# Counting the filler products of TensorE's first gap from the moment when the rows they read exist: 30 matrices in place of 54

## The chip, the core and the metric

The kernel runs on one core of a Trainium2 chip. The metric is device time in microseconds (us) of one execution of the whole program. Before the change three executions took 694.41, 691.67 and 690.75 us, so the median is 691.67 us. Beside them stands one profiled execution, whose trace is what the rest of this document reads.

The core's engines run their own instruction streams in order and wait for each other on semaphores: TensorE (PE in the profile, with its weight loads shown as PEld), VectorE (DVE), ScalarE (ACT), GpSimd (POOL), and SyncE (SP), which here only issues DMAs. DMAs are also issued by POOL and ACT.

## The reference

Two blocks follow each other. The first is a gated recurrence over 768 time steps with a complex decay per channel; batch is 4, there are 8 heads, and the head dimension is 48:

```
scale = min(|a|, 0.999) / (|a| + 1e-6);  a_n = a * scale
S_t = a_n[t] * S_{t-1} + k[t] v[t]^T        (complex state, 48 x 48 per head)
y[t] = q[t] . Re(S_t)
```

The second is a SwiGLU feed-forward on the 3072 rows of the result, each with 384 features (8 heads x 48): an RMS norm with a gain, two matrices 384 x 1536 (`w_gate`, `w_val`), `silu(g) * val`, and one matrix 1536 x 384 (`w_out`). All of it is fp32.

## The kernel before, in words

**Tiling.** The sequence is cut into chunks of 128 steps: 4 x 6 = 24 chunks, numbered n = 0 to 23. Gates are worked out in units: chunks 0 and 1 alone, then pairs of chunks. The feed-forward takes groups of two chunks (256 rows).

**Stages of a chunk.** `load_gates` and `load_kq` (lines 1091 and 1117) fetch the gates `in` and the queries and keys `kin`. `gates` (line 1138) turns the gates into cumulated magnitudes and phases on DVE and ACT and multiplies queries and keys by them: the results are the rows `rot` (one DVE product each for cosine and sine). SP then moves each chunk's `rot` by six DMAs into `kq`, in the layout that the attention needs. `attend` (line 1247) does one chunk's attention on PE: scores (`bank<-kq`, 64 products for a chunk), whose causal part DVE copies into `am`; transposes of the keys (`ident,kq`), copied by ACT into `kt`; the chunk's output (`am,ve` and `kq,state`); the new state (`vn,kt`, 48 products), finished by DVE; and the norm (`ones,sq`, then a power on POOL written to `rs`, spread again by PE as `ident,rs`), after which DVE writes `xT`. `feed` (line 1381) multiplies a group's `xT` by `wg` and `wv`. The values of a chunk are loaded twice, as `ve` and as `vn`; there is one buffer of `vn`, so that the next chunk's load of it waits for the state products of the chunk before.

**The weights** arrive in the inputs' 64-bit form, in pieces of 1536 KB that POOL's DMA queue fetches into the buffers `wo` and `hT` (`fetch`, line 1012). A piece is turned into fp32 by one ACT pass and three DVE passes (`narrow`, line 1035). At most two pieces are under way. Piece 4 (`wo<-in_w_gate_dram` for the second time) also waits until the second chunk's `kq` has landed: POOL reads one element of it (`seen<-kq`), and this read stands on POOL behind the first chunk's power `rs`.

**The order.** Nothing is issued as it is written. Every operation is put down with an engine, an estimated duration, its dependencies and a due time (class `Flow`). `schedule` (line 617) plays the program through with these estimates, engine by engine, and so finds the order in which each engine issues its instructions; `issue` (line 741) emits them in that order. On the chip an engine follows its own order and waits for the semaphores of what it depends on. The planned times themselves are not enforced.

**Fillers.** Where PE would idle in the plan's first 62 us (`WARM`), `schedule` puts products whose result nobody reads (lines 706 to 713): 128x128 by 128x128 in fp32, of the rows `rot` of chunk 0, into a bank of PSUM that is not in use. How many there are comes from the planned gap: its length, less a margin of 0.25 us, by 0.26 us for each. In the trace each of these matrices shows as two MATMUL records. They can't begin before the rows `rot` are written, as they read them. `started` (line 1222) holds one operation, the DVE product that writes those rows; `since` (line 708) is the planned time from which the gap is counted. `recent` is a list of what PE did lately; in the plan, two small groups of products for the decays of chunks 0 and 1 (`bank<-ot,ot`) stand before the first gap, so the list isn't empty there. The fillers stand in PE's stream just ahead of the operation that the plan puts after the gap: here the scores of chunk 0.

Of the kernel before, what the change touches and what calls it, by code (L numbers as in the profile page):

```python
# [500 lines left out]
class Flow:  # L501
# [115 lines left out]
    def schedule(self):  # L617
# [3 lines left out]
        free = {}  # L621
# [10 lines left out]
        recent = []  # L632
# [13 lines left out]
        while True:  # L646
# [58 lines left out]
                dur += self.between(o, last)  # L705
                mode, last = o["mode"], o
            if eng == "PE" and self.warm and not claimed and t < self.warm["until"] and all("end" in x for x in self.warm["after"]):
                since = max([free["PE"]] + [x["end"] + 0.06 for x in self.warm["after"] if not recent])
                step = 0.26 if recent else 0.43
                n = int((t - since - 0.25) / step)  # L710
                if n > 0:
                    self.fillers.append((order - 0.5, n))
                    recent.append((since, since + step * n))
# [1039 lines left out]
```

## Time and profile before

| | before |
|---|---|
| median of three executions | 691.67 us |
| profiled execution | 691.83 us |
| its span | 690.1 us |
| granted TensorE clock, mean | 0.996 |
| busy: PE, DVE, ACT, POOL | 652.9, 556.2, 499.6, 63.7 us |
| bytes moved by DMA | 81.98 MB |

The span runs from the first to the last instruction of the profiled execution; 1.73 us of its own time lie around it. Times in the views count from the span's start. A row of the timeline gives start, duration, engine, the line of the program (746, the line of `issue` from which all is emitted), the operation, what it writes and reads, its shapes and how many like it follow each other; in brackets stands how long the engine was idle before it and what ended that. The duration of a merged row reaches from the first start to the last end. `SPq` and `POOLq` rows are DMA issues: their duration is the issue, not the transfer.

### The profile page before, as it was taken

The page shows a single profiled execution, that of the slowest core. Times are in us where ns is not written, and L with a number is a line of the kernel's source. Part 1 is how long each engine was busy: PE and PEld are TensorE (multiplying, and loading weights), DVE is VectorE, ACT ScalarE, POOL GpSimd, SP SyncE. Part 2 cuts the span into 40 slices and gives each one's busy share as a digit, 9 for nine tenths or more (in the row PEclk, how much of TensorE's full clock was granted, in tenths as well). Part 3 has the DMA queues.
Part 4 walks back from the last instruction along what each step waited for, and adds up shares of the span by engine and source line. Part 5 has one row for each costly group of instructions (what it writes and reads, how often), then busy time and mean ns, then how long its engine had stood idle before and what let it go on. Part 6 is the DMA issues. An engine that isn't in the chain of part 4 may idle for free.

```text
span 690.1 us, 19118 instructions
## 1 busy us (share of the span) xinstructions
PE 652.9 (95%) x7965; PEld 609.6 (88%) x7965; DVE 556.2 (81%) x1026; ACT 499.6 (72%) x864; POOL 63.7 (9%) x109
## 2 busy tenths in 40 slices
PE   0699999999999999999999999989999998999997
PEld 0688887786899999999999999989999998999997
DVE  8969999989998969879989869779879777346563
ACT  8629667895685774874788776867679675799872
POOL 3113031011000100011010100101000000000000
PEclk9999999999999999999999999999999999999999
DMA  9786574355325521354552622556151445735510
GB/s 282 257 230 195 146 208 140 98 128 107 102 54 97 140 34 54 92 117 79 141 89 61 146 53 45 115 107 143 39 107 34 95 128 116 258 95 184 161 47 26
DMA packets 104156, 81.98 MB, mean 119 GB/s; under 512 B 41953, under 2 KB 94561, under 8 KB 104065
## 3 DMA queue, kind: packets, MB, share of 16 engines
q1 hardware_dynamic: 98560, 64.68, 35.0%
q0 software_dynamic: 4416, 15.35, 10.5%
q8 instruction: 63, 1.03, 0.6%
q10 hardware_dynamic: 1088, 0.69, 0.3%
q14 instruction: 29, 0.23, 0.1%
HBM read 55.84 MB, written 4.72 MB: 88 GB/s over the span
## 4 chain that ended last, share of the span: by engine, by line
PE 76%; DVE 8%; issue 4%; SPq 4%; DMA 4%; ACT 3%; POOL 0%; DVEq 0%; POOLq 0%; ACTq 0%
PE bank L746 76%; SPq L746 4%; DVE turns L746 1%; DVE hT L746 1%; DVE t L746 1%; DMA decay<-ends 1%; ACT in L746 1%; ACT t L746 1%; DMA in<-in_w_val_dram 1%; DMA ve<-in_v_dram 1%; DVE rot L746 1%; DVE am L746 1%; ACT L746 1%; DMA vn<-in_v_dram 1%; ACT bank L746 1%
## 5 line engine op out<-in xcount | busy, mean ns | idle before, releaser
L746 PE MATMUL bank<-wo,hT 128*128 128x192 f32 (+1 forms) x696 | 140.7, 350 | 0.0
L746 PEld LDWEIGHTS bank<-wo,hT 128*128 128x128 f32 x696 | 115.0, 190 | 11.6 <-DVE hT L746 0.5
L746 PE MATMUL bank<-xT,wg 128*128 128x128 f32 (+1 forms) x488 | 85.3, 308 | 0.0
L746 PE MATMUL bank<-xT,wv 128*128 128x128 f32 (+1 forms) x488 | 83.2, 303 | 0.0
L746 ACT ACT_TABLE_LOAD x57 | 73.1, 1283 | 9.4 <-DVE rot L746 5.1
L746 ACT ACTIVATE hT<-bank 128x512 f32<-128x512 f32 x100 | 58.4, 596 | 25.0 <-PE bank L746 22.5
L746 PEld LDWEIGHTS bank<-xT,wg 128*128 128x128 f32 x488 | 71.4, 193 | 5.3 <-issue 0.6
L746 PEld LDWEIGHTS bank<-xT,wv 128*128 128x128 f32 x488 | 70.6, 193 | 3.2 <-issue 0.2
L746 POOL TENSOR_TENSOR rs<-ssv,mhalf 128x1 f32<-128x1 f32 x24 | 21.4, 890 | 461.5 <-ACT ssv L746 407.9
L746 DVE COPY_PREDICATED am<-causal,bank 128x512 f32<-128x512 int32 x48 | 34.7, 731 | 22.9 <-PE bank L746 22.8
L746 DVE TENSOR_TENSOR hT<-hT 128x768 f32<-128x768 f32 (+1 forms) x60 | 51.5, 860 | 0.4
L746 PE MATMUL bank<-yg,wg 128*128 128x128 f32 x320 | 50.7, 281 | 0.0
L746 PE MATMUL bank<-yg,wv 128*128 128x128 f32 x320 | 48.8, 275 | 0.0
L746 ACT ACTIVATE bank<-bank 128x512 f32<-128x512 f32 x60 | 35.2, 586 | 17.9 <-PE bank L746 11.4
L746 ACT ACTIVATE sg<-bank 128x256 f32<-128x256 f32 (+1 forms) x72 | 38.5, 536 | 9.2 <-DVE bank L746 4.7
L746 DVE TENSOR_TENSOR hT<-bank,hT 128x512 f32<-128x512 f32 x50 | 34.3, 687 | 13.4 <-ACT bank L746 5.3
L746 PE MATMUL bank<-sums,hT 128*128 128x192 f32 x240 | 44.7, 329 | 0.0
L746 PEld LDWEIGHTS bank<-yg,wg 128*128 128x128 f32 x320 | 42.2, 191 | 1.3 <-issue 0.2
L746 PEld LDWEIGHTS bank<-yg,wv 128*128 128x128 f32 x320 | 42.2, 192 | 0.0
L746 PEld LDWEIGHTS bank<-kq 96*32 96x32 f32 x1536 | 30.5, 110 | 11.2 <-issue 5.1
L746 PEld LDWEIGHTS bank<-sums,hT 128*128 128x128 f32 x240 | 39.1, 190 | 0.4 <-DVE mid L746 0.2
L746 PE MATMUL bank<-kq 96*32 96x128 f32 (+3 forms) x1536 | 36.4, 237 | 3.1 <-DMA decay<-ends 1.9
(217 smaller groups left out, 1451.5 us busy)
## 6 DMA issues: line engine op xcount, KB each, us to landing
kq<-rot SPq DMA_DIRECT2D x84, 128.0 KB, 2.5
kq<-kin SPq DMA_DIRECT2D x60, 128.0 KB, 2.6
kin<-in_q_dram SPq DMA_DIRECT2D x24, 192.0 KB, 2.9
kin<-in_k_dram SPq DMA_DIRECT2D x24, 192.0 KB, 3.3
in<-in_a_re_dram SPq DMA_DIRECT2D x11, 384.0 KB, 4.2
in<-in_a_im_dram SPq DMA_DIRECT2D x11, 384.0 KB, 4.2
out_dram<-ot SPq DMA_DIRECT2D x22, 192.0 KB, 3.0
vn<-in_v_dram SPq DMA_DIRECT2D x20, 192.0 KB, 3.2
```

The source lines that it names most:

```text
L746: fn(*args, **kw)
```

## The change

In `schedule` one condition is taken out of the line that finds the start of a gap. Before, the end of the operations in `started`, plus 0.06 us, counted only if the list `recent` was empty. Now it counts always: a gap starts when PE is free and the rows that the fillers read are there, whichever is later.

```diff
@@ -705,7 +705,7 @@
             if eng == "PE" and self.warm and not claimed and t < self.warm["until"] and all("end" in x for x in self.warm["after"]):
-                since = max([free["PE"]] + [x["end"] + 0.06 for x in self.warm["after"] if not recent])
+                since = max([free["PE"]] + [x["end"] + 0.06 for x in self.warm["after"]])
                 step = 0.26 if recent else 0.43
                 n = int((t - since - 0.25) / step)
                 if n > 0:
```

The emitted program has 30 filler matrices in the first gap in place of 54. The fillers of later gaps and the order of everything else are the same.

## The prediction, as it was made before the changed kernel ran

> **What bounds the kernel now.** I read first which engine is busy in which stretch. Columns of the stretches: from and to, then busy time and count of instructions for PE, PEld, DVE, ACT and POOL, granted clock, DMA share, GB/s.
>
> ```profile
> span 690.1 us, 19118 instructions
> 17.00:25.70 8.70, 2.22 (x13) 2.03 (x13) 7.59 (x15) 8.04 (x10) 1.69 (x3) 1.00 1.02 392
> 25.70:40.00 14.30, 14.30 (x112) 14.18 (x116) 8.96 (x9) 3.55 (x5) 1.70 (x2) 1.00 0.55 141
> 40.00:56.00 16.00, 13.57 (x372) 12.21 (x372) 13.97 (x14) 8.30 (x18) 5.17 (x6) 1.00 0.96 252
> 56.00:82.70 26.70, 26.70 (x171) 24.45 (x170) 26.52 (x37) 20.97 (x26) 5.30 (x4) 1.00 0.53 160
> 200.00:690.00 490.00, 480.03 (x5940) 463.10 (x5939) 375.61 (x741) 355.81 (x640) 29.50 (x47) 1.00 0.41 100
> ```
>
> From 56 us on PE sets the pace (26.70 of 26.70 us, then 480.03 of 490), and in the first of these stretches DVE is as full (26.52). PE is full in 25.70 to 40.00 as well, but there it runs fillers, and DVE (8.96 of 14.30) and ACT (3.55) stand idle. So I look at what they wait for. First PE's timeline:
>
> ```profile
> 25.70 14.31 PE L746 MATMUL bank<-rot 128*128 128x128 f32 x108 [6.37 <-DVE rot L746]
> 39.94 1.33 PE L746 MATMUL bank<-kq 96*32 96x128 f32 x64
> ...
> 42.98 0.86 PE L746 MATMUL bank<-vn,kt 128*32 128x48 f32 x48
> ...
> 45.14 1.33 PE L746 MATMUL bank<-kq 96*32 96x128 f32 x64
> 47.30 0.38 PE L746 MATMUL bank<-ident,rs 128*128 128x128 f32 x1 [0.82 <-POOL rs L746]
> ...
> 52.49 0.82 PE L746 MATMUL bank<-vn,kt 128*32 128x48 f32 x43
> 54.51 0.28 PE L746 MATMUL bank<-vn,kt 128*32 128x48 f32 x5 [1.19 <-issue]
> ```
>
> The fillers are 108 records, two for each of 54 matrices. They begin when DVE has written `rot`, 6.37 us after PE became free, and hold PE until 39.94, when chunk 0's scores start. Now the other engines in that time, and last one row of the chain of waits:
>
> ```profile
> 25.67 3.82 SPq L746 DMA_DIRECT2D kq<-rot  x6
> 31.61 0.49 POOL L746 COPY seen<-kq 96x1 f32<-96x1 f32 x1 [2.92 <-DMA kq<-rot]
> 33.71 0.95 DVE L746 TENSOR_SCALAR wv<-hT 128x1536 int32<-128x1536 int32 x1
> 40.80 1.37 DVE L746 COPY_PREDICATED am<-causal,bank 128x512 f32<-128x512 int32 x2 [6.14 <-PE bank L746]
> 41.79 0.89 ACT L746 ACTIVATE kt<-bank 128x384 f32<-128x384 f32 x2 [11.78 <-PE bank L746]
> ```
> ```profile
> 28.89 2.49 DMA kq<-rot
> ```
>
> Chunk 0's `kq`, all that its scores read, has landed by 31.4 (28.89 + 2.49; POOL reads it at 31.61). The scores start 8.5 us later, and nothing but the fillers ahead of them in PE's stream explains it. DVE waits 6.14 us and ACT 11.78 us for the products behind. So the end of the fillers sets this stage.
>
> **Does the code do what it says?** 54 fillers at 0.26 us each and a margin of 0.25 mean a planned gap of 14.29 to 14.55 us; 30 mean 8.05 to 8.31. The difference, 5.98 to 6.50, should be the time from PE free to `rot` written. The trace has 6.37 for it. So the 24 matrices taken out are the ones that fitted into a time when the fillers could not yet run. What they read doesn't change, so the remaining 30 start at 25.70 again.
>
> **What the removed fillers cost.** Their pace isn't even:
>
> ```profile
> L746 PE MATMUL bank<-rot x15: 421/421/582, 25.7 to 28.8; 128*128 128x128 f32 x15
> 33.48 6.53 PE L746 MATMUL bank<-rot 128*128 128x128 f32 x57
> ```
>
> The first 15 records start at 25.7 to 28.8, one per 3.1 / 14 = 0.221 us. The last 57 take from 33.48 to 39.94, when the scores start: 6.46 / 57 = 0.113 us each. The 48 records that go come off the end: 48 x 0.1133 = 5.44 us. (The mean pace, 14.24 / 108 x 48 = 6.33, would count slow ones that stay.) The scores of chunk 0 then start at 39.94 - 5.44 = 34.50, still 3.1 after `kq` landed, and DVE's `am`, which follows their start by 0.86, at 35.36. DVE is free at 34.66 (33.71 + 0.95), so it loses nothing of the 5.44.
>
> **What may not follow by 5.44.** All that hangs on PE, DVE and ACT moves with the scores, as the order is the same. Held back can only be what SP and POOL had under way. The rows are the issues of chunk 1's `kq`, the last load of `kin`, `vn` for chunk 1, and under each its time to landing (least, median, most):
>
> ```profile
> L746 SPq DMA_DIRECT2D kq<-rot x6: 547/598/1590, 32.9 to 37.1; - x6
> DMA to landing us min/median/max: 2.3/2.5/3.5
> ```
> ```profile
> 40.85 0.49 SPq L746 DMA_DIRECT2D kin<-in_k_dram  x1
> ```
> ```profile
> DMA to landing us min/median/max: 5.3/5.3/5.5
> ```
> ```profile
> 43.88 0.34 SPq L746 DMA_DIRECT2D vn<-in_v_dram  x1
> ```
> ```profile
> DMA to landing us min/median/max: 4.7/4.7/4.7
> ```
>
> *Chunk 1's `kq`.* Its last DMA is issued at 37.1 and lands at 39.4 to 40.6. The scores of chunk 1 would be due at 45.14 - 5.44 = 39.70, so PE may wait 0 to 0.9 us. That wait is nearly hidden:
>
> ```profile
> 45.06 1.75 DVE L746 SCALAR_TENSOR_TENSOR wv<-hT,wv 128x1536 int32<-128x1536 int32 x1
> 46.72 1.32 DVE L746 COPY_PREDICATED am<-causal,bank 128x512 f32<-128x512 int32 x2
> ```
>
> DVE takes the scores only after the pass over `wv`, at 46.72 - 5.44 = 41.28; scores that start by 41.28 - 0.86 = 40.42 cost it nothing, and at 40.6 it loses 0.2. PE's next step, spreading `rs`, waits for POOL until 47.30 - 5.44 = 41.86, and 40.6 + 1.33 is 41.93. I take 0.1, with 0 and 0.2 as bounds.
>
> *`vn` of chunk 1.* Its load waits until chunk 0's state products have read the buffer (43.84), and then SP is free. With the change that is so at 38.4, but SP's stream stands at the loads of `kin` ahead of it until 41.34 (40.85 + 0.49). So `vn` is issued at 41.4, only 2.5 us earlier. With its own 4.7 us it lands at 46.1; behind `kin`, which lands at 46.35, I put it at 46.4 or later. The longest landing of this stretch is that of a `ve` load:
>
> ```profile
> DMA to landing us min/median/max: 2.1/4.9/7.4
> ```
>
> By it the late bound is 48.8. The state products of chunk 1 are due at 52.49 - 5.44 = 47.05. Before, they ended at 54.79 with a stall of 1.19 us that the profile can put down to nothing ("issue"); chunk 0's 48 took 0.86. To keep the 5.44 they must end by 49.35, so without the stall they may begin as late as 48.49. The terms: -1.2 if the stall goes and `vn` is there in time, 0 if a late `vn` just fills the stall's place, +1.75 if `vn` lands at 48.8 and a stall comes on top. I take +0.2, near the middle case: rows show neither.
>
> *Other stalls of that name.* In all of the run PE has three:
>
> ```profile
> PE bank L746 <- issue: 3.6, 3, 2.1
> ```
>
> The change shifts all that follows in PE's stream by 48 products and 48 loads of weights. Whether these stalls move with it no row shows; for a price I take the row's own bound of 2.1 either way, and 0 as the value.
>
> *Weights.* POOL's queue and what it feeds:
>
> ```profile
> 45.05 2.20 POOL L746 TENSOR_TENSOR rs<-ssv,mhalf 128x1 f32<-128x1 f32 x1 [12.95 <-ACT ssv L746]
> 47.22 0.17 POOL L746 COPY seen<-kq 96x1 f32<-96x1 f32 x1
> 47.33 0.80 POOL L746 DMA_DIRECT2D wo<-in_w_gate_dram  x1
> ...
> 55.73 0.57 POOL L746 COPY junk<-wo 1x1 int32<-1x1 int32 x1 [0.75 <-DMA wo<-in_w_gate_dram]
> ```
> ```profile
> 58.60 1.65 ACT L746 ACTIVATE wo<-wo 128x1536 int32<-128x1536 uint32 x1
> ```
>
> Piece 4 is issued behind the power `rs`, which moves with ACT, and behind `seen<-kq`, which needs chunk 1's `kq` (by 40.6). So it goes out at 47.33 - 5.44 = 41.89, and by its 8.4 us lands at 50.3; ACT wants it at 58.60 - 5.44 = 53.16. It has 2.9 us to spare, as before: 0.
>
> *Behind 56 us.* Every load is issued on a buffer that PE, DVE or ACT set free, so it moves with them, and PE and DVE are full. The 5.44 isn't given back: 0.
>
> **Sum.** On the profiled execution's own time: 691.83 - 5.44 + 0.1 + 0.2 = 686.7 us. Of that time 1.73 lie outside the span, so the span would be 685.0. The median of the runs is 0.16 lower than this execution; I forecast 686.6. Its own range: down to 691.83 - 5.44 - 1.2 = 685.2, up to 691.83 - 5.44 + 0.2 + 1.75 = 688.3.
>
> **Rivals.** *DMA becomes the bound of the stage* (0.14). For it: DMAs keep their engines busy for a share of 0.96 from 40 to 56 us, and the loads of `kin` go out no earlier, while `vn` and piece 4 are pushed on top of them. If all behind `vn` can move only as its issue does, by 43.88 - 41.34 = 2.54, the time is 691.83 - 2.54 = 689.3. It needs `vn` to land at 52.49 - 2.54 = 49.95, 8.6 us after its issue. Against it: 7.4 is the longest in this stretch, and piece 4 comes 0.5 us behind `vn`. The Trainium skill speaks for it: by DMA: Bandwidth & Descriptors, section "Issuing engines are not separate DMA queues", DMAs of SP, ACT and POOL end up interleaved on the same 16 DMA engines, so `vn` would share them with piece 4. No row before shows the two together.
>
> *PE falls back to its slow pace* (0.05), the rival on the other side. Place: chunks 0 and 1, the stretch 40 to 56 before. The 15 slow records came after 6.37 us of idling. If fewer fillers and waits for `kq` or `vn` leave PE in that state, its 13.57 us of work there run at 0.221 against 0.113, 1.95 times as long: +12.9, and 691.83 - 5.44 + 12.9 = 699.3. It turns the result once more than 5.44 / 0.95 = 5.7 us of work run slow. Against it: the 30 fillers still last 8.8 us, the fast pace is there well before 33.48, and the waits expected are 0.9 and 1.75 us, far from 6.37. The Trainium skill, TensorE: Matmul & The Clock Gate, section "HAM oscillation — how this bites in real kernels", puts the fall of the clock at idle gaps above about 3.4 us. By that rule the decisive gap is shorter than the one that this trace shows, but still not reached. The granted clock reads 1.00 in the slow stretch too, so only the products' own durations would show it.
>
> *The gap isn't shortened* (0.02): another number of fillers, or the scores held by something else. Then it is 691.8. The arithmetic of the gap above speaks against it.
>
> **How the numbers follow.** The forecast has 0.79. A difference from no change can be told above about 0.5%, which is 3.46 us here: faster means below 688.2. The forecast's range lies there but for its last 0.1; the DMA rival and the unshortened gap fall within 0.5%, the slow pace beyond. So faster 0.79, same 0.16, slower 0.05. For 8 times in 10 the range takes in the forecast's own and reaches to the DMA rival: 684.9 to 689.4. I leave out the slow pace, the unshortened gap, and stalls that move by more than 1.2 us.
>
> **What would show it.** Right: 60 filler records from 25.7, scores at 34.4 to 34.6, DVE idle 0.7 before `am`; chunk 1's scores at 39.7 to 40.6; `vn` issued at 41.4; chunk 1's state products done by about 49.4; the rest of the trace earlier by the same amount. Wrong: PE waiting for `vn` beyond 48.5, ACT waiting for piece 4 at 53, products of 421 ns after 34.5, or new stalls called issue of 2 us and more in the first 60 us.

## The result, and the profile after

Four executions of the changed kernel took 682.97, 684.83, 685.51 and 685.98 us: a median of 685.17 against 691.36 us before, a ratio of 0.9899 with a 95% interval of 0.9866 to 0.9931. On the 691.67 us of before that ratio makes 684.7, just under the forecast's range (684.9 to 689.4), which had 686.6 as its value. Two later series of twelve executions each gave 0.9948 (0.9920 to 0.9976) and 0.9939 (0.9917 to 0.9961). The 28 executions together have a median of 686.75 us.

The first trace after the change is that of its fastest execution (682.97 us, span 681.2). Its stretches, with the columns of the first fence of the prediction:

```profile
span 681.2 us, 19019 instructions
25.70:35.20 9.50, 9.50 (x61) 9.38 (x62) 8.94 (x9) 3.46 (x5) 1.45 (x2) 1.00 0.55 141
35.20:51.40 16.20, 13.92 (x374) 12.43 (x374) 14.07 (x15) 8.27 (x18) 4.41 (x5) 1.00 0.95 248
51.40:77.00 25.60, 24.03 (x159) 22.29 (x158) 24.32 (x33) 19.18 (x25) 3.03 (x4) 1.00 0.59 170
```

The filler stretch is 9.5 us long and not 14.3, with the same work of DVE and ACT in it. The stretch of chunks 0 and 1 is as long as before (16.2 against 16.0). The one that follows isn't full any more: PE is busy for 24.03 of 25.60 us. PE's timeline shows why:

```profile
25.67 9.59 PE L746 MATMUL bank<-rot 128*128 128x128 f32 x60 [6.36 <-DVE rot L746]
35.19 1.33 PE L746 MATMUL bank<-kq 96*32 96x128 f32 x64
...
40.40 1.33 PE L746 MATMUL bank<-kq 96*32 96x128 f32 x64
42.55 0.49 PE L746 MATMUL bank<-ident,rs 128*128 128x128 f32 x2 [0.82 <-POOL rs L746]
...
45.78 0.31 PE L746 MATMUL bank<-kq,state 96*32 96x128 f32 x3 [0.97 <-issue]
...
49.10 0.88 PE L746 MATMUL bank<-vn,kt 128*32 128x48 f32 x48 [0.35 <-DMA vn<-in_v_dram]
...
51.36 2.84 PE L746 MATMUL bank<-xT,wg 128*128 128x128 f32 x24
...
63.81 2.86 PE L746 MATMUL bank<-xT,wg 128*128 128x256 f32 x12 [1.57 <-ACT sg L746]
```

The 60 records are there. The scores start 4.75 us earlier (35.19 for 39.94), and so do the products behind them, up to 51.36. The first 256-wide products, at 66.98 before, are only 3.17 us earlier: PE waits 1.57 us for ACT. ACT, in turn, waited for piece 4 of the weights, which POOL had issued 4.75 us earlier than before:

```profile
42.58 0.80 POOL L746 DMA_DIRECT2D wo<-in_w_gate_dram  x1
```
```profile
55.41 1.68 ACT L746 ACTIVATE wo<-wo 128x1536 int32<-128x1536 uint32 x1 [1.50 <-DMA wo<-in_w_gate_dram]
```

It took 12.8 us to land, where it had taken 8.3 before. DVE's idle time before `am`, 6.14 us before, has shrunk to 1.42:

```profile
36.05 1.36 DVE L746 COPY_PREDICATED am<-causal,bank 128x512 f32<-128x512 int32 x2 [1.42 <-PE bank L746]
```

From there to 440 us the lead stays below 3.9 us. Then it grows to 8.7, at two places where the first trace before the change had waits and this one has hardly any: 2.14 us at 464, put down to issue, and 1.93 us for a DMA at 572, which was followed by slow products. The same place after the change, at 565.10, has a wait of 0.36 us. The two rows of before are these:

```profile
464.24 0.52 PE L746 MATMUL bank<-ident,kq 96*128 96x96 f32 x4 [2.14 <-issue]
...
572.22 0.99 PE L746 MATMUL bank<-kq 96*32 96x128 f32 x32 [1.93 <-DMA decay<-ends]
```

Whether this second part of the lead belongs to the change was the first question for the experiments.

### The profile page after: what moved, and what is told of

Same layout as the page of the kernel before. It is cut to its first block, busy times and chain, and to the rows that moved or that the text cites. A ratio compares the mean times of both kernels' runs of the same rounds, so it can differ in the third digit from the quotient of the medians.

```text
span 681.2 us, 19019 instructions
## 1 busy us (share of the span) xinstructions
PE 646.5 (95%) x7914; PEld 603.4 (89%) x7917; DVE 556.8 (82%) x1026; ACT 499.4 (73%) x864; POOL 66.8 (10%) x109
## 3 DMA queue, kind: packets, MB, share of 16 engines
q0 software_dynamic: 4416, 15.35, 10.9%
q8 instruction: 63, 1.03, 0.6%
## 4 chain that ended last, share of the span: by engine, by line
issue 33%; PE 32%; DVE 13%; DMA 9%; ACT 7%; POOL 2%; SPq 2%; POOLq 0%; DVEq 0%; ACTq 0%
PE bank L746 32%; DMA sq<-rs 4%; SPq L746 2%; ACT L746 2%; DMA wo<-in_w_gate_dram 2%; DVE hT L746 2%; DVE turns L746 2%; ACT t L746 1%; DVE wo L746 1%; POOL rs L746 1%; DVE rot L746 1%; DVE t L746 1%; ACT in L746 1%; DVE wv L746 1%; DVE wg L746 1%
## 5 line engine op out<-in xcount | busy, mean ns | idle before, releaser
L746 PE MATMUL bank<-yg,wv 128*128 128x128 f32 x320 | 48.8, 275 | 0.0
L746 ACT ACTIVATE turns<-in 128x768 f32<-128x768 f32 (+1 forms) x39 | 30.6, 792 | 11.2 <-DVE in L746 5.8
```

Of the source, the lines that this page charges most:

```text
L746: fn(*args, **kw)
```

## The experiments

The table gives for every kernel the number of fillers in the first gap, its executions with their median and the ratio to the kernel before, and three times from its one trace: the start of chunk 0's scores, of the first products of `xT` and `wg`, and of the first 256-wide ones.

| run | fillers | executions, median us | ratio (95%) | scores | `xT,wg` | 256-wide |
|---|---|---|---|---|---|---|
| before | 54 | | | 39.94 | 56.17 | 66.98 |
| n54_again | 54 | 1, 691.59 | | 40.11 | 56.98 | 67.77 |
| n54_third | 54 | 12, 690.27 | 0.9982 (0.9962 to 1.0002) | 39.48 | 56.73 | 67.68 |
| after | 30 | 4, 685.17 | 0.9899 (0.9866 to 0.9931) | 35.19 | 51.36 | 63.81 |
| n30_again | 30 | 12, 687.46 | 0.9948 (0.9920 to 0.9976) | 34.70 | 50.97 | 62.52 |
| n30_third | 30 | 12, 687.16 | 0.9939 (0.9917 to 0.9961) | 34.97 | 54.73 | 65.45 |
| n20 | 20 | 12, 685.35 | 0.9916 (0.9891 to 0.9941) | 32.84 | 54.11 | 65.26 |
| n30_calm2 | 30 | 6, 685.32 | 0.9911 (0.9885 to 0.9937) | 34.84 | 54.27 | 64.99 |
| n54_calm2 | 54 | 12, 690.55 | 0.9991 (0.9968 to 1.0014) | 40.07 | 56.45 | 67.17 |
| n20_calm2 | 20 | 6, 684.30 | 0.9893 (0.9869 to 0.9917) | 33.13 | 54.03 | 65.24 |
| n30_tiny | 30 | 1, 681.25 | | 35.09 | 50.12 | 61.82 |
| n30_tiny_timed | 30 | 9, 685.24 | 0.9911 (0.9877 to 0.9945) | 34.87 | 56.85 | 68.15 |
| n54_tiny | 54 | 1, 693.63 | | 39.03 | 55.99 | 67.01 |
| n30_calm2_tiny | 30 | 12, 686.78 | 0.9929 (0.9896 to 0.9961) | 35.60 | 50.65 | 61.37 |
| n25_calm2_tiny | 25 | 12, 685.50 | 0.9923 (0.9893 to 0.9953) | 33.10 | 55.33 | 66.50 |

### How much of the difference repeats

The kernels before and after, unchanged, traced twice more each. Their expectations:

> The kernel before, traced a second time. In the first trace PE stood still for 2.14 us at 464 (put down to issue) and for 1.93 us at 572 (a DMA of the decays), and ran slowly for some 3 us after the second; the changed kernel's trace has neither, and its lead grows there from 3.85 to 8.7 us. Theory A, these stalls come and go from one execution to the next: at least one of the two is missing here, or stands at another place, and the span is 2 to 5 us shorter than 690.1 if both are missing. Theory B, they belong to where the 54 fillers put the rest of the program: both are there again, within 0.5 us of 2.14 and 1.93, and the span is within 1 us of 690.1.

> The changed kernel, traced and timed again. What should repeat under both theories is the lead at the front: the first scores 4.7 to 5.5 us before 39.94, and then a wait of PE of about 1.6 us in front of the 256-wide products on xT and wg, since ACT waits for piece 4 of the weights. That leaves 3.1 us. Theory A: later stalls of 1 to 2 us appear here at other places, and the gain over five rounds is 3 to 6 us (ratio 0.991 to 0.996). Theory B: no stall behind 100 us over 0.7 us, and the gain is 7 to 9 us (0.987 to 0.990).

> The kernel before, timed against itself and traced a third time. The ratio holds 1.000 in its interval; how far it lies from it shows what twelve executions can tell. In the trace, theory F: the stall put down to issue is after product record 475 or 347, or there is none. Theory A: the waits of 2 us at 464 and 572 of the first trace are there, gone or elsewhere, and the span follows them.

> The changed kernel once more. Four executions gave a ratio of 0.9899 (0.9866 to 0.9931), twelve others 0.9948 (0.9920 to 0.9976). Theory S, both are scatter about the gain at the front, 3.1 to 4.8 us: the ratio is 0.9915 to 0.9955, and the intervals of all three hold 0.993. Theory B, the gain is the 1% first measured and the second was disturbed: below 0.991. In its trace the first products on xT and wg start at 50.9 to 51.4 if chunk 1's keys and queries land by 40.6, later if they don't.

The stall at 464 is in neither of the other traces with 54 fillers: theory B falls for it. The wait at 572 isn't bound to the 54 fillers either. It appears with 30 as well, here in the timeline of n30_again, as does the slow pace behind it:

```profile
566.40 1.30 PE L746 MATMUL bank<-kq 96*32 96x128 f32 x32 [2.55 <-DMA decay<-ends]
567.63 1.22 PE L746 MATMUL bank<-xT,wg 128*128 128x128 f32 x4
```

In this place the traces with 54 fillers wait 1.92 to 2.40 us, those with 30 between 0.36 and 2.55, most often 1 to 2. So the first trace after the change was the lucky one in this place, and of the 8.7 us that it led by at the end, some 5 came from waits that differ from one execution to the next. The spans of the three traces with 54 are 690.1, 689.9 and 691.1 us, of those with 30 681.2, 684.0 and 684.0.

The ratios say the same. Theory S had the third series at 0.9915 to 0.9955; it came out at 0.9939, and the intervals of the three series have 0.992 to 0.993 in common. The kernel before, timed against itself, came out at 0.9982 with 1.000 in its interval: twelve executions leave an error of about 0.2%. About 0.993, or 4.8 us, is what the change brings.

Where the scatter comes from shows in the granted clock. In short windows it reads 0.50 behind some of the waits, for 3.4 or 6.8 us, and 1.00 around them. These are rows of the first trace before, behind its wait at 572, and of n30_third, behind a stall of 2.22 us in chunk 1, for which its first products of `xT` and `wg` came at 54.73 and not at 50.9 to 51.4 (columns as in the first fence of the prediction; the third number from the end is the clock):

```profile
572.60:576.00 3.40, 3.40 (x36) 3.23 (x26) 1.64 (x3) 0.75 (x2) 0.53 (x1) 0.50 0.72 53
```
```profile
47.70:54.50 6.80, 6.80 (x75) 6.67 (x76) 2.94 (x5) 5.56 (x11) 1.33 (x2) 0.50 1.09 311
```

The mean granted clock is on record for every execution, traced or not, and the time follows it. Of the 95 executions of the kernel before in the later series, the 30 at 0.999 or 1.000 have a median of 689.7 us, the 19 at 0.994 or less 693.7. Of the 28 of the changed kernel, 5 at 0.999 have 684.9, 13 at 0.994 or less 688.2. So at a like clock the two kernels lie some 5 us apart. The first four executions of the changed kernel had 0.997 to 0.999; its later 24 had 0.995 in the mean, the 95 of before 0.997. The changed kernel loses the clock more often, and by the relation between clock and time that costs it about 1 us. For the executions without a trace this is a correlation.

The front repeats better. The scores start 4.9 us earlier in the mean of three traces each (34.95 for 39.84), the first 256-wide products 3.5 us (63.93 for 67.48). The 4.8 us of the ratio agree with that within their error of some 2 us. The three traces with 54 fillers also wait longer behind 460 us: some 4 us in the places at 464 to 476 and 572 together, those with 30 fillers 1.0 to 3.3, but n54_calm2 only 2.5. Whether a part of this belongs to the change stays open.

### What sets the stage now: fewer fillers

```diff
-                    self.fillers.append((order - 0.5, n))
+                    self.fillers.append((order - 0.5, n if self.fillers else 20))
```

> 20 fillers in the first gap, all else as in the changed kernel. They would end at about 33, after chunk 0's keys and queries have landed (31.4). Theory P, PE's fillers still set this stage: the first scores come 2.3 us earlier than with 30, and the time falls by another 1.5 to 2.3 us. Theory D, the DMAs set it now: chunk 1's keys and queries (39.4 to 40.6), vn (48.7) and piece 4 of the weights (55.4) land no earlier, PE waits for them by as much more as the scores came earlier, and the time is within 0.7 us of that with 30 fillers.

The scores came 2.1 us earlier than the 34.95 of 30 fillers, and nothing was left of it: the products of `xT` and `wg` started at 54.11, later than in two of the three traces with 30. The timeline of n20 shows the waits that took the place of the fillers:

```profile
39.40 1.57 PE L746 MATMUL bank<-kq 96*32 96x128 f32 x64 [0.59 <-DMA kq<-rot]
...
46.12 0.30 PE L746 MATMUL bank<-kq,state 96*32 96x128 f32 x1 [2.33 <-issue]
...
49.96 1.50 PE L746 MATMUL bank<-vn,kt 128*32 128x48 f32 x48 [1.23 <-DMA vn<-in_v_dram]
51.39 1.22 PE L746 MATMUL bank<-rot 128*128 128x128 f32 x4
```

Chunk 1's `kq` and `vn` land no earlier, as theory D had it. Behind the first of the two long waits, from 48.1 to 55.0, the granted clock was 0.50 and PE ran at its slow pace: 1.22 us for four filler records against 0.69 otherwise. The ratio, 0.9916, can't be told from that of 30 fillers.

### Why piece 4 is late: loads that crowd it

The first attempt moved the load of `vn` for chunk 2 forward past seven loads. Its expectation says that nothing is left out; that was wrong. The load then overwrote the values that chunk 1's state products still had to read, so that the state of chunk 1 was made of chunk 2's values. It measured another program, with a wait of 4.02 us for this load, and says nothing on the theory (ratio 1.0005, 0.9979 to 1.003).

```diff
+    loads = {n: [o for o in flow.ops if o["stage"] == ("attend", n) and o["eng"] == "SP"][-1] for n in (1, 2)}
+    loads[2]["order"] = loads[1]["order"] + 0.25
```

> As the changed kernel, but on SP the load of vn for chunk 2, which waits until chunk 1's state products are done at about 50, is put ahead of seven loads (the real gates of the fourth unit and values ve of chunks 2 and 3), so that these go out after 50 and not at 42 to 49, beside vn of chunk 1 and piece 4 of the weights. Nothing is left out. Theory D, these loads crowd out piece 4: it lands about 8.4 us after its issue (near 51) and not 12.9 us (55.4), ACT's wait of 1.50 us for it and PE's of 1.57 us are gone, and the time falls by 1 to 2 us below the changed kernel's. If piece 4 is late for another reason: it lands at 54 to 56 again, and the time is the same or up to 1 us worse.

The second moves the seven loads back behind it; every load reads and writes what it did.

```diff
+    between = [o for o in flow.ops if o["eng"] == "SP" and loads[1]["order"] < o["order"] < loads[2]["order"]]
+    for o in between:
+        o["order"] = loads[2]["order"] + 0.4 * (o["order"] - loads[1]["order"]) / (loads[2]["order"] - loads[1]["order"])
```

> The changed kernel with seven loads on SP moved: the real gates of the fourth unit and values ve of chunks 2 and 3 go out behind the load of vn for chunk 2, so after about 50 us and not at 42 to 49. (The run before this one moved the load of vn forward past them; that made it overwrite the values that chunk 1's state products still had to read, so it measured another program. Here every load reads and writes what it did.) Piece 4 of the weights took 12.1 to 13.1 us to land in the traces with 30 and 20 fillers, 8.4 and 8.6 with 54. Theory D, these loads crowd it: it lands 8.4 to 10 us after its issue at about 42, ACT does not wait for it, PE does not wait for ACT in front of the first 256-wide products, and these start about 0.7 to 1.6 us earlier than in the changed kernel's traces (63.8 and 62.5); the time falls by 0.5 to 2 us. Otherwise: it lands at 54 or later as before, and the time is the same.

> The same seven loads moved in the kernel before, with its 54 fillers. Theory D: nothing waited for piece 4 there (it landed 2.9 us before ACT took it), so the time is that of the kernel before within 0.3% and the first 256-wide products start at 67 to 68. If the moved loads help by themselves, behind the front: it is faster by 1 us or more.

> 20 fillers and the seven loads moved. Theory D: the wait of 1.23 us for vn of chunk 1 shrinks or goes, and with it the slow products behind it; the first 256-wide products start at 61 to 62, and the time is 1 to 3 us below that of 30 fillers alone. If chunk 1's keys and queries (landing at 39.4) set the stage by now: no more than 0.5 us below 30 fillers with the loads moved.

With 30 fillers and the loads moved piece 4 landed 10.0 us after its issue, and PE doesn't wait for ACT in front of the 256-wide products. POOL's and ACT's rows in n30_calm2:

```profile
42.24 0.80 POOL L746 DMA_DIRECT2D wo<-in_w_gate_dram  x1
...
52.33 0.80 POOL L746 COPY junk<-wo 1x1 int32<-1x1 int32 x1 [0.43 <-DMA wo<-in_w_gate_dram]
```
```profile
55.44 1.65 ACT L746 ACTIVATE wo<-wo 128x1536 int32<-128x1536 uint32 x1
```

Over all traces with 20 to 30 fillers it took 10.9 to 13.2 us with the loads in their place (six traces) and 9.0 to 11.1 with them moved (four), 12.2 and 10.2 in the mean. So these loads account for about 2 us of the delay, and with them moved it is still longer than the 8.3 to 8.6 of the three traces of the kernel before. The missing wait in n30_calm2 proves nothing by itself: in this execution the stall put down to issue was 1.87 us, the products behind it ran at the slow pace, and the first products of `xT` and `wg` came only at 54.27, so that ACT and PE were late too. For the same reason the forecast of earlier 256-wide products failed, and so it did with 20 fillers: n20_calm2 has a stall of 2.06 us, still waits 1.09 us for `vn`, and comes to the 256-wide products at 65.24. Two later traces without that stall, n30_tiny and n30_calm2_tiny, show the effect, on one trace each: with the loads in place piece 4 takes 10.9 us, ACT waits 0.89 us for it and PE 0.82 for ACT; with them moved it takes 9.0 and neither waits. ACT's and PE's rows, n30_tiny first:

```profile
53.42 1.67 ACT L747 ACTIVATE wo<-wo 128x1536 int32<-128x1536 uint32 x1 [0.89 <-DMA wo<-in_w_gate_dram]
61.82 2.86 PE L747 MATMUL bank<-xT,wg 128*128 128x256 f32 x12 [0.82 <-ACT sg L747]
```
```profile
52.97 1.62 ACT L747 ACTIVATE wo<-wo 128x1536 int32<-128x1536 uint32 x1
61.37 2.82 PE L747 MATMUL bank<-xT,wg 128*128 128x256 f32 x12
```

In the kernel before the move changes nothing (0.9991), as nothing waited for piece 4 there. The ratios with 30 and 20 fillers, 0.9911 and 0.9893, come from six executions each, and their intervals touch that of n30_third: a gain in time by the move alone isn't shown.

### The stall called issue

In both first traces with 54 fillers this stall stands after the same product, the 43rd of chunk 1's state products. Counted from the start of PE's records that is the 475th: 12 + 108 + 64 + 8 + 32 + 48 + 6 + 4 + 64 + 2 + 4 + 64 + 4 + 6 + 6 + 43. With 30 fillers it stands in chunk 1's output, after 12 + 60 + 64 + 8 + 32 + 48 + 6 + 4 + 64 + 2 + 4 + 43 = 347, with 20 after 347 again. The difference is 128. To move the work against that count, small records were put ahead of the fillers; they run while PE is idle:

```diff
+    flow.warm["first"] = [(nc.tensor.matmul, (banks[3][0:1, 0:1],), dict(lhsT=ones, rhs=ones, start=True, stop=True))] * 10
...
+        steps.append((self.fillers[0][0] - 0.1, self.warm["first"]))
```

> The changed kernel with 10 products of one column (20 records) ahead of the 30 fillers; they read a constant, so they run while PE is idle before 25.7 and cost nothing. In both traces with 54 fillers PE has its stall put down to issue after its 475th product record (the 43rd of chunk 1's state products), in those with 30 and with 20 fillers after its 347th, which is 128 earlier. Theory F: PE's instructions arrive in blocks of 128 products, and the stall is a late block. Then it is after the 347th record again, the 20 new ones counted: 20 products earlier in the work than with 30 fillers, after the 23rd of chunk 1's 64 output products and not after the 43rd. Rival, something that the chunk waits for and the profile doesn't show: it stays after the 43rd of them.

> The kernel before, 54 fillers, with the same 20 records ahead. Theory F2: the packet of instructions that started at 51.9 and 52.8 in the two traces with 54 belongs to a place 20 products earlier in the work now; PE is busy there without a long wait, so the packet starts only some 0.5 us earlier and a stall remains, of 0.5 to 1.7 us, after the 23rd of the 48 state products of chunk 1 and not after the 43rd. If the stall is tied to the work and not to the packets: after the 43rd again.

> The kernel with 30 fillers and 20 small records ahead of them, timed. In its one trace the stall put down to issue in chunk 1 is gone, not moved by 20 products as theory F had it. Theory F2: the stall ends 2.5 to 3.0 us after a packet of the instruction queue starts (42.8 with 30 fillers, 40.4 with the 20 records), so it appears only where the packet starts late; 20 records more bring this packet forward past the wait for rs, and this repeats: no stall called issue over 0.3 us between 35 and 60, the first products on xT and wg at about 50.1 and not 51.0 to 51.4, and the time 0.8 to 1.5 us below that of 30 fillers alone (ratio 0.990 to 0.994). Chance: the stall is there again, and the ratio is that of 30 fillers alone, 0.9948 within 0.001.

With 30 fillers the stall was not moved but gone, and this execution, at 681.25 us, is among the fastest of all. With 54 it moved to where the count puts it, though not to the 475th: n54_tiny stops in chunk 1's scores, after record 348 by the trace, one off from the others. In the third trace of the kernel before it stands at 347 too, after one of the two `ident,rs` records (12 + 108 + 64 + 8 + 32 + 48 + 6 + 4 + 64 + 1). First n54_tiny, then n54_third:

```profile
44.17 1.05 PE L747 MATMUL bank<-kq 96*32 96x128 f32 x46
47.16 0.53 PE L747 MATMUL bank<-kq 96*32 96x32 f32 x18 [1.94 <-issue]
```
```profile
48.48 0.27 PE L746 MATMUL bank<-ident,rs 128*128 128x128 f32 x1 [1.28 <-issue]
```

So the stall goes with a place in PE's stream of instructions, not with the work. n54_calm2 has no such stall in chunk 1 at all. The profile lists an instruction queue among the DMAs; this is its row for the whole run and, behind it, for the stretch 42.8 to 42.9 of the trace after the change (packets, MB, share of 16 engines):

```profile
q8 instruction: 63, 1.03, 0.6%
```
```profile
q8 instruction: 1, 0.02, 84.6%
```

63 packets of 1.03 MB are 16 KB each; PE's 7965 products of the run before, in blocks of 128, would make 62.2. In every trace with this stall one of them starts shortly before, and PE goes on 2.5 to 3.0 us after its start: 51.9 and 54.51 before, 42.8 and 45.78 after, 43.5 and 46.12 with 20 fillers, 44.4 and 47.16 in n54_tiny, 45.6 and 48.48 in n54_third, and likewise in five more. Where the packet starts early enough there is no stall: 40.4 in n30_tiny, with the 347th product at about 44.3. That PE waits for these packets is an inference, but ten stalls agree on the delay and, but for n54_tiny's one record, on the place.

Timed, the 20 records gave 0.9911. The trace taken then shows no such stall either, as theory F2 had it, but it isn't early: chunk 1's `kq` landed late and PE waited for it, and then for `vn`.

```profile
42.36 1.33 PE L747 MATMUL bank<-kq 96*32 96x128 f32 x64 [2.29 <-DMA kq<-rot]
...
52.70 1.50 PE L747 MATMUL bank<-vn,kt 128*32 128x48 f32 x48 [2.44 <-DMA vn<-in_v_dram]
```

### All remedies together

> 30 fillers, the 20 records, and the seven loads behind the load of vn for chunk 2. If the two remedies are separate: no stall called issue in chunk 1, no slow products at 47 to 54, no wait for piece 4; the first products on xT and wg at 50, the first 256-wide ones at 60.8 to 61.2 in place of 61.8 to 63.8; ratio 0.987 to 0.991. If moving the loads gives nothing once the stall is gone: the ratio of the 20 records alone, within 0.001.

> As the one before with 25 fillers and 30 records ahead, so that everything behind has the same place in PE's stream. First scores about 1.1 us earlier, near 33.9. Theory D, chunk 1's keys and queries set the stage now (they land at 39.4 to 40.2): its scores start no earlier than 39.4, so at most 0.6 us is gained, ratio within 0.001 of the one with 30.

In its traced execution (682.24 us) n30_calm2_tiny has the front that was expected: products of `xT` and `wg` at 50.65, 256-wide ones at 61.37, no stall called issue and no wait for piece 4. Over twelve executions its ratio is 0.9929, that of the change alone. But these twelve fall into two groups: five with a granted clock of 0.999 or 1.000 took 681.2 to 683.4 us, seven with 0.994 or 0.995 took 686.7 to 690.0. Where the clock held, the remedies may be worth some 2 us against the 684.9 of the changed kernel, on five executions each; where it didn't, nothing. In the trace of n25_calm2_tiny, an execution with a clock of 0.991, the scores of chunk 1 waited 1.62 us for `kq` until 40.72 and the state products 2.55 for `vn`. No version beats the changed kernel in its median by more than this measurement can tell.

## Why the prediction was right or wrong, point by point

**What bounds the front: right.** PE's fillers held everything, and taking 24 of them away moved scores, DVE and ACT forward. The code does what was said: 60 records instead of 108.

**The removed fillers, 5.44 us: right in kind, 4.9 measured.** The forecast took all 48 records at the fast pace of the tail and the slow start as fixed. The scores start 13.9 to 14.7 us after the fillers in the three traces with 54, 9.2 to 9.5 with 30; the 60 records that stay were to take 8.8. The slow start isn't the same length from one execution to the next. The Trainium skill has a reason that these numbers agree with but don't prove: by TensorE: Matmul & The Clock Gate, section "What's actually happening", the clock gate looks at windows that run freely, so that the length of the slow start depends on where in a window the first product falls.

**Chunk 1's `kq`, 0.1 us with a bound of 0.2: right in the three traces with 30 fillers, too narrow a bound.** They have no wait for it; n30_tiny_timed has 2.29 us. One trace's landing times (2.3 to 3.5 us) were taken for the spread of all.

**`vn`, +0.2 between -1.2 and +1.75: the landing was later than said, and the cost within the bounds by another way.** It was to land at 46.4 to 48.8. It landed 7.5, 6.8 and 8.0 us after its issue in the three traces, at about 49.0, 48.4 and 49.9, where the trace before had 4.7 us. In the first PE waited for it until 49.10, beyond the 48.5 that the prediction had named as a sign of being wrong, though only for 0.35 us. What was not seen is that the stall goes with the stream of instructions: it didn't go or stay, it came 128 products earlier, as 0.97 to 2.22 us in chunk 1's output.

**Weights, 0: wrong, the step of the mechanism that failed.** Piece 4 was said to land 8.4 us after its issue, with 2.9 us to spare. It took 12.0 to 13.2 in the three traces. In the first ACT waited 1.50 us for it and PE 1.57 for ACT, in n30_again 0.43 and 0.67; in n30_third nobody waited, as PE was late by itself. So it took 1.6 us of the lead in the first trace and 0.7 in the second. The 8.4 us were those of a load issued 4.75 us later; brought forward, it met seven loads of SP from their first on. The pair n30_tiny and n30_calm2_tiny showed that moving these takes the wait away. The rival of the DMAs had this mechanism, but was asked to explain the whole result and so got only 0.14. What the page cited for it says of DMAs interleaving on the same engines (DMA: Bandwidth & Descriptors of the Trainium skill) agrees with this. The step made the time longer, so it doesn't explain a time below the range.

**Behind 56 us 0, other stalls 0, and both left out of the range: the step that put the time under it.** The sum had the rest of the trace earlier by the same amount. In the first trace the lead was 3.17 us at 66.98 and 3.85 at 444, and then grew by 4.9 at two places whose instructions are the same: the stall of 2.14 us at 464 was gone, and at 572 the wait of 1.93 us had shrunk to 0.36, without the 3.4 us at a clock of 0.50 behind it. The prediction had listed a stall of this name and size, priced it at 2.1, valued it at 0 and kept it out of the range. The other traces with 54 fillers don't have the stall at 464, and n30_again has both the wait and the fall of the clock, at 566: executions of one kernel differ by these. Whether the shift of PE's stream had a part in the stall at 464 isn't shown. The four executions of the first result had a clock of 0.997 to 0.999 and so few such falls. That they came out 0.2 us under the range was luck. The two series of twelve stand at 688.1 and 687.5 on the same base, within it, and the some 5 us between the kernels at a like clock are what was forecast (5.1). Why the three executions without a trace were fast isn't shown beyond their clock.

**The slow pace, 0.05 with 699.3: it came, at a far lower price.** In three of the seven traces with 30 fillers in the table (n30_third, n30_calm2, n30_tiny_timed) the granted clock fell to 0.50 between 44 and 59 us. With 54 fillers this happened in two of five, for 3.4 us each. In n30_third it lasted 6.8 us, with products of 421 ns, another sign that the prediction had named, and the products of `xT` and `wg` came at 54.73 and not at 51.2; the 256-wide ones came 1.6 and 2.9 us later than in the two other traces, as PE would then have waited for ACT anyway. Two readings failed here. The prediction held the waits too short to matter against the 6.37 us of the only example that it knew, but its own trace had another: 3.4 us at 0.50 behind the 1.93 us of 572, lost in the mean of 1.00 over 200 to 690 us. And it expected that the clock column would not show a slow stretch. That is so at the start of the fillers (1.00 with products of 421 ns) but not later. The Trainium skill (TensorE: Matmul & The Clock Gate, section "HAM oscillation — how this bites in real kernels") has idle gaps above about 3.4 us as the bound. That is not what was seen here, and the measurement decides: the longest single waits at the falls were 1.3 to 2.9 us.

## What to carry to other kernels

Filler work that keeps a clock up belongs inside the time in which the engine would idle anyway; count it from the moment when its own inputs exist, or it delays what it was to help. A stage that is brought forward meets the transfers that used to be finished before it: take a transfer's time from a stretch as crowded as the one it moves into. And one trace of each kernel can differ by 5 us in waits that neither edit caused, so that a gain of 1% is read at places in the trace, over several executions, and not from two spans. Look at the granted clock of each execution beside its time, and in windows of a few us: a mean of 1.00 over a long stretch hides a fall.

## What the runs showed of the hardware

PE has stalls that go with the count of instructions ahead of them. In ten traces they stood after product record 475 or 347 (348 in one), 128 apart, each ending 2.5 to 3.0 us after a 16 KB packet of the instruction queue began. With twenty tiny records ahead in idle time three traces with 30 fillers had no such stall.

PE's granted clock falls to 0.50 for 3.4 or 6.8 us at a time in these traces (but for the last microsecond of one, and n30_calm, where it lasted 10.2). The longest single waits at the falls were 1.3 us (n54_third, at 48) to 2.9 us (n54_tiny, at 475). The length of one wait doesn't decide it: behind 2.34 us (n54_again, at 573) and 2.14 us (before, at 464) the clock stayed at 1.00. A 128x128 fp32 record takes 421 ns at the slow pace and 275 at the other. At the first fillers, which run at the slow pace too, the column reads 1.00.

A transfer of 1536 KB by POOL's queue took 8.3 to 8.6 us in the three traces of the kernel before. Issued some 5 us earlier, beside more loads of SP, it took 10.9 to 13.2, and 9.0 to 11.1 with seven of these loads out of its way.
